# Induced attention and maxout on one core: loads cut into four pieces, two output buffers, a later fetch

## The chip, the cores and the metric

The kernel runs on one core of a Trainium2 chip. The metric is the device time of one execution in microseconds (us), lower is better. TensorE is called PE, ScalarE ACT, VectorE DVE, GpSimd POOL, and SyncE SP, as in the profile. SP issues nearly all transfers (DMAs) of this kernel.

## The reference, cut to what matters

```
B, N, m, C = 4, 12544, 32, 128                      # x: B x N x C, inducing I: m x C
def mab(q, kv):
    s = scale * (q @ kv.transpose(0, 2, 1));  s = s - s.max(-1, keepdims=True)
    a = np.exp(s);  a /= a.sum(-1, keepdims=True) + 1e-09
    return a @ kv
h = mab(I, x)                                       # phase one: 32 rows for each batch
x2 = mab(x, h)                                      # phase two: every token
out = np.maximum(np.maximum(x2 @ w1, x2 @ w2), x2 @ w3) @ w_out    # d_ff = 768
```

All values are float32.

## The kernel before, in words

**Tiles.** Each batch has 98 tiles of 128 tokens, in a short group of 2 tiles and six full groups of 16. The maxout uses `max(w1, w2, w3) = w2 + max(w1 - w2, w3 - w2, 0)` folded with `h`, so that a chunk of up to 512 tokens is worked in six **slots**, one for each block of 128 of the 768 hidden channels. A full group is four chunks, 24 slots, and is called a **window** here; windows are numbered 0 to 23 over the four batches, six a batch, and the short group's chunk stands ahead of each batch's first window.

**A slot.** PE makes two products of the chunk's probabilities `pT` (`pu`, L756; `pv`, L762). ACT turns `pu` into `ru` (a rectifier, L771), DVE takes the maximum with `pv` (`h`, L789), ACT rounds it to a short float (`hi`, L778), and POOL or DVE makes the rest (`lo`, L786, L792). Six slots later PE adds three products into `acc` (L812 to L814, `stage2`; L811 at a chunk's start). After a chunk's last slot, `finish` lets ACT copy `acc` to an output tile `o` (L819), and SP sends `o` to memory (L820, 256 KB).

**What stands beside the slots.** The list `plan` holds for each slot the other steps, put there by `at(slot, step)`. Everything is recorded in this order, and each engine works its own instructions strictly in it. Chunk k's `pT` is written by four DMAs of 64 KB (L741, `probs`) that are recorded in slot 6(k-2)+4; they read `ph` and `pl` of the chunk's group, which ACT (L718) and DVE (L721) write for a whole group at the window's offsets 14 and 15. `ph` and `pl` may be written only when the DMAs that read the tiles before them have landed.

Batches 1 to 3 have their phase one worked during the batch before, a **turn** for each group (windows 0 to 15; 18 turns, two each in windows 0 and 1). With s a turn's first slot, at offset 2 (or 15) of its window: products at s (L363), negated maxima at s+2, `turn_send` at s+4 writes the maxima of 128 rows to memory (`far`, L400, 512 bytes in pieces of 4), `turn_fetch` reads them back so that each row gets four of them (`mm`, L407, 2 KB), and `turn_least`, `turn_weights` and `turn_transpose` follow at s+19 to s+22. `turn_sums` (L446) multiplies the group's tokens in the next window's burst. After a batch's last turn, `turn_totals` and `combine_...` make the next batch's `h`, and `combine_rows` lays its products out by 16 DMAs (`us`, L656, four at each of offsets 18, 20, 22 and 24 of windows 4, 10 and 16).

**Loads.** A group comes twice: with tokens in the partitions (`xg`, L95, 1 MB, `load_tokens`, wanted by `turn_sums`) and with channels there (`xT`, L106, 1 MB, `load_channels`, wanted by the turn's products and later by the scores, L673). For batches 2 and 3 the plan is:

```
at(window(i - 1) + 15, load_channels, n, k)
at(window(i) + 17, load_tokens, n, k)
```

**SP's queue.** The built program gives the DMAs eight semaphores in turn (`DMAHW0` to `DMAHW7`), and a DMA is not issued before the one eight issues earlier has landed. The rows below show it as `[waits DMAHW...]`. SP issues in order, so an issue that waits holds back all behind it.

**The output tile.** `op.tile(..., bufs=3)` asks for three, but the automatic allocation put all 100 at one address: in the built program each copy (L819) waits for the DMA of the chunk just before it.

Of the kernel before, what the change touches and what calls it, by code (L numbers as in the profile page):

```python
# [8 lines left out]
F32 = mybir.dt.float32  # L9
# [16 lines left out]
def kernel(ctx, tc, x, xt, ind_t, w1, w2, w3, w_out, out):  # L26
    nc = tc.nc
    B, N, C = x.shape
    M = ind_t.shape[1]
    DF = w1.shape[1]  # L30
    P = 128
# [3 lines left out]
    GT = 16  # L35
    XB = 5
    XTB = 8
    MANUAL = {mybir.EngineType.PE, mybir.EngineType.Activation, mybir.EngineType.SP, mybir.EngineType.DVE, mybir.EngineType.Pool}

    LOADS = (0, 7, 1, 2, 8, 3, 9, 4, 10, 5)  # L40
# [9 lines left out]
    UW = 2 * DF + C  # L50
# [3 lines left out]
    groups = []  # L54
    t0 = 0
    while t0 < NT:
        nt = NT % GT if t0 == 0 and NT % GT else GT
        assert nt == GT or nt <= NQ
        g = dict(t0=t0, nt=nt, at=t0 * P)
# [8 lines left out]
    const = ctx.enter_context(tc.tile_pool(name="const", bufs=1))  # L68
    xp = ctx.enter_context(tc.tile_pool(name="xp", bufs=2))
    wk = ctx.enter_context(tc.tile_pool(name="wk", bufs=2))  # L70
    bp = ctx.enter_context(tc.tile_pool(name="bp", bufs=2))
    hp = ctx.enter_context(tc.tile_pool(name="hp"))
    op = ctx.enter_context(tc.tile_pool(name="op", bufs=2))
    dp = ctx.enter_context(tc.tile_pool(name="dp", bufs=2, space=bass.MemoryType.DRAM))
    ps = ctx.enter_context(tc.tile_pool(name="ps", bufs=1, space=PSUM))

# [7 lines left out]
    xv = x.rearrange("b (p t) c -> b p t c", t=NT)  # L84


    def load_group(b, gi, pieces=1):
        g = groups[gi]
        if g["nt"] == GT:
            xg = xgs_free.pop(0)  # L90
        else:
            xg = xp.tile([P, g["nt"], C], F32, name="xgs", tag="xgs", bufs=1)
        n = g["nt"] // pieces
        for k in range(0, g["nt"], n):
            nc.sync.dma_start(out=xg[:, k : k + n, :], in_=xv[b, :, g["t0"] + k : g["t0"] + k + n, :])  # L95
        return xg

    def load_group_t(b, gi):
        g = groups[gi]
        n = g["nt"] * P  # L100
        if g["nt"] == GT:
            xT = xts_free.pop(0)
        else:
            xT = short_t[b % 2]
        if b >= B - xt.shape[0]:
            nc.sync.dma_start(out=xT, in_=xt[b - B + xt.shape[0], :, g["at"] : g["at"] + n])  # L106
        return xT

    xg_next = {}
    xts_free = [const.tile([P, GT * P], F32, name=f"xT{i}", tag=f"xT{i}") for i in range(XTB)]  # L110
    xgs_free = [const.tile([P, GT, C], F32, name=f"xg{i}", tag=f"xg{i}") for i in range(XB)]
    w_space = xts_free.pop()
    shelf = const.tile([P, UW + 2 * groups[0]["nt"] * P + 2 * P + 2 * M], F32, name="shelf")
    shelf_at = [0]

    def place(n):
        shelf_at[0] += n
        return shelf[:, shelf_at[0] - n : shelf_at[0]]

    short_t = [place(groups[0]["nt"] * P) for i in range(2)]  # L120
    iT = place(M)

# [8 lines left out]
    def first_loads():  # L131
# [13 lines left out]
        out=sel[:, :M], in_=ident.rearrange("p (q m) -> p m q", m=M), axis=AX.X, op=ALU.add  # L145
    )
    nc.vector.tensor_copy(
        out=sel[:, M:].rearrange("p (q m) -> p q m", m=M),
        in_=sel[:, :M].unsqueeze(1).to_broadcast([P, NQ - 1, M]),
# [88 lines left out]
    state = {}  # L238
# [15 lines left out]
        st["xg"][gi] = xg_next.pop((b, gi))  # L254
        st["xT"][gi] = load_group_t(b, gi)

    def load_tokens(b, k):
        for gi in turns[k]:
            state[b]["xg"][gi] = load_group(b, gi)

    def load_channels(b, k):
        for gi in turns[k]:
            state[b]["xT"][gi] = load_group_t(b, gi)

    def transpose_x(b, gi, k):
        st = state[b]
# [213 lines left out]
    def phase1_first(weights):  # L480

        start_batch(0)
        nc.sync.dma_start(out=iT, in_=ind_t)
        nc.scalar.mul(out=iT, in_=iT, mul=scale)
        first_loads()
        def work(n):
            for _ in range(n):
                next(weights, None)

        def half(gi, k):  # L490
            if gi < NG:
                if k == 0:
                    start_group(0, gi)
                    if gi == NG - 1:
                        start_batch(1)
                        load_channels(1, 0)
                for i in (k, k + 4):
                    transpose_x(0, gi, i)

        start_group(0, 0)  # L500
        transpose_x(0, 0, 0)
        attend_products(0, 0, bank_a[0])
        attend_max(0, 0)
        attend_column(0)
        attend_spread(0, bank_o[0])
        attend_least(0, 0)
        half(1, 0)
        half(1, 8)
        work(4)
        for gi in range(NG - 1):  # L510
            attend_products(0, gi + 1, bank_a[(gi + 1) % 2])
            attend_weights(0, gi)
            half(gi + 2, 0)
            attend_max(0, gi + 1)
            attend_column(0)
            half(gi + 2, 8)
            if gi > 0:
                attend_sums(0, gi - 1, bank_o[1])
                attend_keep(0, gi - 1)
                if xgs_free and (0, NG - 1) not in xg_next and NG - 1 not in state[0]["xg"]:  # L520
                    xg_next[(0, NG - 1)] = load_group(0, NG - 1)
            attend_transpose(0, gi)
            work(WORK[gi][0])
            if gi == NG - 3:
                transpose_w2()
            if gi == NG - 2:
                prep_products()
            attend_spread(0, bank_o[0])
            attend_least(0, gi + 1)
            work(WORK[gi][1])  # L530
        attend_weights(0, NG - 1)
        attend_sums(0, NG - 2, bank_o[1])
        attend_keep(0, NG - 2)
        combine_least(state[0])
        combine_weights(state[0])
        attend_transpose(0, NG - 1)
        combine_mask(state[0])
        sum_groups(state[0])
        attend_sums(0, NG - 1, bank_o[1])
        combine_groups(state[0], range(NG - 1), bank_u[0])  # L540
        total_sums(state[0], bank_o[0])
        attend_keep(0, NG - 1)
        invert_total(state[0])
        combine_groups(state[0], range(NG - 1, NG))
        combine_states(state[0], NQ)
        for _ in weights:
            pass
# [267 lines left out]

    def finish(c):
        at = groups[c.gi]["at"] + (c.q or 0) * c.w
        o = op.tile([P, 512], F32, name="o", tag="o", bufs=3)
        nc.scalar.copy(out=o[:, : c.w], in_=c.acc[:, : c.w])  # L819
        nc.sync.dma_start(out=out[c.b, :, at : at + c.w], in_=o[:, : c.w])  # L820

# [23 lines left out]
    def at(s, f, *args):  # L845
        plan[s].append((f, args))
# [13 lines left out]
    def turn(b, k, s):  # L860

        at(s, turn_products, b, k)
        at(s + 2, turn_max, b, k)
        at(s + 4, turn_send, b, k)
        at(s + 11, turn_fetch, b, k)
        at(s + 19, turn_least, b, k)
        at(s + 20, turn_weights, b, k)
        at(s + 22, turn_transpose, b, k)

    def window(i):  # L870
        return (i // (NG - 1)) * per_batch + short + (i % (NG - 1)) * WIN
# [1 line left out]
    NW = NG - 1  # L873
    FIRST = ((0, 0), (0, 1), (1, 0), (1, 1), (2, 0), (3, 0))
    BURST = (2, 15)
    LOADT = ((0, 0, 0), (0, 0, 1), (0, 5, 2), (0, 15, 3), (1, 16, 4), (2, 15, 5))
    LOADX = ((0, 4, 0), (0, 17, 1), (1, 4, 2), (1, 17, 3), (2, 17, 4), (3, 17, 5))

    for i in range(B * NW):
        b, g = i // NW, i % NW + 1  # L880
# [9 lines left out]
    for n in range(1, B):  # L890
        for k in range(NK):
            if n == 1:
                i, part = FIRST[k]
                then = (i + 1, part)
                if k > 0:
                    at(window(LOADT[k][0]) + LOADT[k][1], load_channels, n, LOADT[k][2])
                at(window(LOADX[k][0]) + LOADX[k][1], load_tokens, n, LOADX[k][2])
            else:
                i, part = NW * (n - 2) + NW - 2 + k, 0
                then = (i + 1, part)  # L900
                if k == 0:
                    at(window(i - 1) + 7, start_batch, n)
                at(window(i - 1) + 15, load_channels, n, k)
                at(window(i) + 17, load_tokens, n, k)
            at(window(then[0]) + BURST[then[1]], turn_sums, n, k)
            at(window(then[0]) + BURST[then[1]] + 1, turn_keep, n, k)
        st = ("state", n)
        s0 = window(NW * n - 2)
        at(s0 + 6, turn_totals, n, bank_a[1])
        at(s0 + 7, invert_total, st)  # L910
        at(s0 + 8, combine_states, st, 1)
        at(s0 + 15, combine_products, n, bank_a[1])
        at(s0 + 15, scores_products, n, 0, bank_a[1][:, UQ : UQ + 2 * M])
        at(s0 + 16, combine_high, st)
        at(s0 + 17, combine_low, st)
        for r in range(NQ):
            at(s0 + 18 + 2 * r, combine_rows, st, r)
        softmax2(n, 0, *(s0 + k for k in (17, 18, 19, 20, 21, 22, 23, 24, 26, 28)))
# [116 lines left out]
```

## Time and profile before

| | |
|---|---|
| time, three runs | 865.87, 865.97, 873.05 us (median 865.97) |
| the profiled execution | 871.83 us, of which the span from the first to the last instruction is 870.0 us |
| granted PE clock over the span | 0.982 |
| PE / ACT / DVE / POOL busy | 94% / 85% / 74% / 73% of the span |
| DMA | 102.54 MB, 118 GB/s on average |

A busy share is an average over the whole span. What a stage is limited by is read from the waits of that stage: which engine stood idle before which instruction, and what ended it. "A <- B" in a row of waits says that A's engine stood idle until B released it.

### The profile page before, as it was taken

The numbers are of one execution on the slowest core, as the hardware profiler recorded it, in microseconds if no ns is written. First come the engines' busy times: TensorE is split into PE (matmuls) and PEld (weight loads), VectorE is DVE, ScalarE is ACT, GpSimd is POOL, SyncE is SP. The second block draws the span as 40 slices with busy tenths as digits, with TensorE's granted clock in tenths as the row PEclk, the third lists the DMA queues.
The fourth block names the chain that finished last, engine by engine and source line by source line (L and its number), as shares of the span: only waits on it lengthen the run. The fifth ranks groups of instructions, "written<-read, shape, count | busy, mean of one in ns | idle before, by whom it ended". The sixth has DMA issues, their size and how long they took to land.

```text
span 870.0 us, 14626 instructions
## 1 busy us (share of the span) xinstructions
PE 819.8 (94%) x4530; PEld 631.8 (73%) x4530; DVE 642.9 (74%) x1112; ACT 741.5 (85%) x1508; POOL 632.3 (73%) x509
## 2 busy tenths in 40 slices
PE   6878999998998998998998999999999999999998
PEld 4645777686776767767766776687777887778786
DVE  6857687686766777867776687687788788778865
ACT  5657798896877889889787897898999999999997
POOL 0037687695776768769677696697788898878887
PEclk9979999999999999999999999999999999999999
DMA  9315552533534245255253433534423222222221
GB/s 347 151 46 185 165 174 74 170 120 101 160 98 146 71 142 166 66 158 157 68 168 95 159 107 106 164 96 130 121 71 103 74 68 67 79 73 73 65 81 49
DMA packets 48813, 102.54 MB, mean 118 GB/s; under 512 B 14304, under 2 KB 18016, under 8 KB 43488
## 3 DMA queue, kind: packets, MB, share of 16 engines
q1 hardware_dynamic: 48736, 101.62, 37.6%
q8 instruction: 36, 0.59, 0.4%
q14 instruction: 41, 0.34, 0.2%
HBM read 48.16 MB, written 25.70 MB: 85 GB/s over the span
## 4 chain that ended last, share of the span: by engine, by line
PE 61%; DMA 20%; ACT 10%; DVE 5%; SPq 2%; issue 2%; POOL 0%; DVEq 0%; ACTq 0%; POOLq 0%
PE pu L756 11%; PE acc L812 11%; PE pv L762 10%; PE acc L813 10%; PE acc L814 10%; DMA pT<-pl 8%; DMA pT<-ph 6%; DMA out_dram<-o 4%; ACT ru L771 4%; ACT hi L778 3%; PE aux L673 3%; DMA xg<-in_x_dram 2%; SPq L741 2%; PE acc L446 2%; PE acc L811 2%; PE aux L363 2%
## 5 line engine op out<-in xcount | busy, mean ns | idle before, releaser
L786 POOL TENSOR_TENSOR lo<-h,hi 128x512 fp32r<-128x512 f32 (+1 forms) x498 | 627.0, 1289 | 180.4 <-ACT hi L778 130.0
L789 DVE TENSOR_TENSOR h<-pv,ru 128x512 f32<-128x512 f32 (+1 forms) x600 | 403.4, 675 | 191.3 <-PE pv L762 107.5
L771 ACT ACTIVATE ru<-pu 128x512 f32<-128x512 f32 (+1 forms) x600 | 369.9, 616 | 63.7 <-PE pu L756 60.1
L778 ACT CAST hi<-h 128x512 fp32r<-128x512 f32 (+1 forms) x600 | 380.6, 634 | 6.9 <-DVE h L789 6.4
L756 PE MATMUL pu<-pT,us 128*128 128x512 f32 (+1 forms) x600 | 236.0, 394 | 32.2 <-DMA pT<-pl 17.5
L812 PE MATMUL acc<-hi,wo_hi 128*128 128x512 f32 (+1 forms) x600 | 236.8, 395 | 0.0
L762 PE MATMUL pv<-pT,us 128*128 128x512 f32 (+1 forms) x600 | 234.8, 391 | 1.9 <-DVE h L789 1.9
L813 PE MATMUL acc<-hi,wo_lo 128*128 128x512 f32 (+1 forms) x600 | 233.1, 389 | 0.0
L814 PE MATMUL acc<-lo,wo_hi 128*128 128x512 f32 (+1 forms) x600 | 232.8, 388 | 0.0
L756 PEld LDWEIGHTS pu<-pT,us 128*128 128x128 f32 x600 | 113.9, 190 | 63.9 <-ACT ru L771 15.2
L812 PEld LDWEIGHTS acc<-hi,wo_hi 128*128 128x128 f32 x600 | 114.0, 190 | 43.4 <-issue 20.9
L762 PEld LDWEIGHTS pv<-pT,us 128*128 128x128 f32 x600 | 114.2, 190 | 27.6 <-DVE h L789 6.2
L814 PEld LDWEIGHTS acc<-lo,wo_hi 128*128 128x128 f32 x600 | 113.8, 190 | 23.5
L813 PEld LDWEIGHTS acc<-hi,wo_lo 128*128 128x128 f32 x600 | 114.0, 190 | 22.3
L819 ACT COPY o<-acc 128x512 f32<-128x512 f32 (+1 forms) x100 | 60.2, 602 | 21.2 <-DMA out_dram<-o 18.1
L792 DVE TENSOR_TENSOR lo<-h,hi 128x512 fp32r<-128x512 f32 x102 | 73.8, 724 | 0.7 <-ACT hi L778 0.7
L811 PE MATMUL acc<-pT,us 128*128 128x512 f32 (+1 forms) x100 | 39.4, 394 | 0.0
L234 POOL TENSOR_TENSOR wo_lo<-xT,wo_hi 128x768 fp32r<-128x768 f32 x1 | 1.8, 1808 | 37.7 <-ACT wo_hi L233 37.7
L673 PE MATMUL aux<-xT,hT 128*32 128x512 f32 x192 | 26.4, 623 | 0.0
L721 DVE TENSOR_TENSOR pl<-aux,ph 128x512 fp32r<-128x512 f32 x24 | 16.5, 688 | 9.9 <-ACT ph L718 9.6
L446 PEld LDWEIGHTS acc<-xg,aT 128*32 128x32 f32 x576 | 16.6, 110 | 8.8 <-issue 4.8
L718 ACT CAST ph<-aux 128x512 fp32r<-128x512 f32 x24 | 14.9, 621 | 9.3 <-DMA pT<-ph 5.0
(132 smaller groups left out, 448.6 us busy)
## 6 DMA issues: line engine op xcount, KB each, us to landing
out_dram<-o SPq DMA_DIRECT2D x96, 256.0 KB
xg<-in_x_dram SPq DMA_DIRECT2D x23, 1024.0 KB
xT<-in_xt_dram SPq DMA_DIRECT2D x18, 1024.0 KB
pT<-ph SPq DMA_DIRECT2D x192, 64.0 KB
pT<-pl SPq DMA_DIRECT2D x192, 64.0 KB
raw<-in_w_dram SPq DMA_DIRECT2D x3, 768.0 KB
us<-uh SPq DMA_DIRECT2D x24, 52.0 KB
us<-ul SPq DMA_DIRECT2D x24, 52.0 KB
```

Of the source, the lines that this page charges most:

```text
L756: nc.tensor.matmul(out=pu[:, :w], lhsT=state[c.b]["us"][:, 2 * j * P : (2 * j + 1) * P], rhs=c.pT[:, :w], start=True, stop=True)
L762: nc.tensor.matmul(out=pv[:, : d.w], lhsT=state[d.b]["us"][:, (2 * j + 1) * P : (2 * j + 2) * P], rhs=d.pT[:, : d.w], start=True, stop=True,)
L771: nc.scalar.activation(out=ru[:, :w], in_=pu[:, :w], func=AF.Relu)
L778: nc.scalar.copy(out=hi[:, : c.w], in_=h[:, : c.w])
L786: nc.gpsimd.tensor_sub(**args)
L789: nc.vector.tensor_max(out=h[:, : d.w], in0=pv[:, : d.w], in1=relus.pop(s)[:, : d.w])
L792: nc.vector.tensor_sub(**low)
L811: nc.tensor.matmul(out=c.acc[:, :w], lhsT=us[:, 2 * DF :], rhs=c.pT[:, :w], start=True, stop=False)
L812: nc.tensor.matmul(out=c.acc[:, :w], lhsT=wo_hi[:, j, :], rhs=c.hh[j][:, :w], start=False, stop=False)
L813: nc.tensor.matmul(out=c.acc[:, :w], lhsT=wo_lo[:, j, :], rhs=c.hh[j][:, :w], start=False, stop=False)
L814: nc.tensor.matmul(out=c.acc[:, :w], lhsT=wo_hi[:, j, :], rhs=c.hl[j][:, :w], start=False, stop=(j == NJ - 1))
L819: nc.scalar.copy(out=o[:, : c.w], in_=c.acc[:, : c.w])
```

## The change: what it does

There are three edits. Every load of tokens or channels of a full group is cut into four DMAs of 256 KB, and the pieces are put at slots of their own (for batches 2 and 3: channels at offsets 5, 8, 11, 14 of the window before the turn's, where one DMA stood at 15; tokens at 7, 12, 17, 22 of the turn's window, where one stood at 17). `o` is no longer a pool's tile: the chunks take two fixed 512-element stretches of the constant tile `shelf` in turn. `turn_fetch` moves from s+11 to s+12. New line numbers: `pT` L763, `xg` L271, `xT` L282, copy L841, output L842, `far` L421, `mm` L428, `us` L678, sums L467.

```diff
-    def load_tokens(b, k):
+    def load_tokens(b, k, piece):
         for gi in turns[k]:
-            state[b]["xg"][gi] = load_group(b, gi)
+            g = groups[gi]
+            if piece == 0:
...
+            n = g["nt"] // PIECES
+            if n or piece == 0:
+                cut = slice(piece * n, (piece + 1) * n) if n else slice(0, g["nt"])
+                nc.sync.dma_start(out=state[b]["xg"][gi][:, cut, :], in_=xv[b, :, g["t0"] :, :][:, cut, :])
...
-        o = op.tile([P, 512], F32, name="o", tag="o", bufs=3)
+        o = outs[c.n % OB]
...
-        at(s + 11, turn_fetch, b, k)
+        at(s + 12, turn_fetch, b, k)
...
-    LOADT = ((0, 0, 0), (0, 0, 1), (0, 5, 2), (0, 15, 3), (1, 16, 4), (2, 15, 5))
-    LOADX = ((0, 4, 0), (0, 17, 1), (1, 4, 2), (1, 17, 3), (2, 17, 4), (3, 17, 5))
+    LOADT = ((0, 0), (0, 1), (0, 13), (0, 17), (1, 17), (2, 5))
+    LOADX = ((0, 5), (0, 17), (1, 5), (1, 17), (2, 9), (3, 7))
...
-                at(window(i - 1) + 15, load_channels, n, k)
-                at(window(i) + 17, load_tokens, n, k)
+                for piece in range(PIECES):
+                    at(window(i - 1) + 5 + 3 * piece, load_channels, n, k, piece)
+                    at(window(i) + 7 + 5 * piece, load_tokens, n, k, piece)
```

`load_channels` is cut in the same way; for batch 1 its pieces stand 2 slots apart and those of the tokens 3 apart, from the offsets in `LOADT` and `LOADX` (window, offset).

**First place: SP's queue in window 13** (a turn of batch 3), from the output of the chunk that ends at offset 6 on. Before:

```order
L820 DMA out_0_dram<-o_6401 128x512 [waits DMAHW4_49,Activation_49]
L400 DMA far_6404<-mq_6371 4x32x1 [waits DMAHW5_49,DVE_49]
L741 DMA pT_6463<-ph_6127 32x512 [waits DMAHW6_49,PE_49]
L741 DMA pT_6463<-pl_6142 32x512 [waits DMAHW7_49]
...
L820 DMA out_0_dram<-o_6497 128x512 [waits DMAHW2_49,Activation_49]
L407 DMA mm_4664<-far_6404 128x1x4 [waits DMAHW5_49,DMAHW3_49]
L106 DMA xT6_92<-in_xt_dram 128x2048 [waits DMAHW4_49]
L741 DMA pT_6559<-ph_6529 32x512 [waits PE_49,Activation_49]
L741 DMA pT_6559<-pl_6544 32x512 [waits DMAHW6_49,DVE_49]
...
L95 DMA xg1_95<-in_x_dram 128x2048 [waits DMAHW1_49]
L820 DMA out_0_dram<-o_6592 128x512 [waits DMAHW2_49,Activation_49]
```

The same place now:

```order
L421 DMA far_6440<-mq_6407 4x32x1 [waits DMAHW3_49,DVE_49]
L271 DMA xg1_92<-in_x_dram 128x512 [waits DMAHW4_49]
L282 DMA xT6_89<-in_xt_dram 128x512 [waits DMAHW5_49,PE_49]
L763 DMA pT_6501<-ph_6163 32x512 [waits DMAHW6_49,PE_49]
...
L282 DMA xT6_89<-in_xt_dram 128x512 [waits DMAHW2_49]
L842 DMA out_0_dram<-shelf_96 128x512 [waits DMAHW3_49,Activation_49]
L271 DMA xg1_92<-in_x_dram 128x512 [waits DMAHW4_49]
L282 DMA xT6_89<-in_xt_dram 128x512 [waits DMAHW5_49]
L428 DMA mm_4642<-far_6440 128x1x4 [waits DMAHW6_49]
L763 DMA pT_6598<-ph_6567 32x512 [waits DMAHW7_49,PE_49,Activation_49]
...
L271 DMA xg1_92<-in_x_dram 128x512 [waits DMAHW3_49]
```

Two pieces now stand between `far` and the four `pT` behind it. The next output is now the eighth issue after `far` and waits for `far`'s semaphore (`DMAHW3` in both rows); before, it was the fifth. Two pieces stand ahead of `mm`, and no 1 MB load stands behind it.

**Second place: SP's queue in window 4**, where `combine_rows` lays out batch 1's products beside the turn of batch 2's first group. Here `xg2` (16 tiles of that group) is loaded, its last piece being this row now:

```order
L842 DMA out_0_dram<-shelf_96 128x512 [waits DMAHW2_49,Activation_49]
L678 DMA us_2734<-uh_2698 32x416 [waits DMAHW3_49,PE_49]
...
L763 DMA pT_2803<-ph_2654 32x512 [waits DMAHW3_49,PE_49]
...
L678 DMA us_2734<-ul_2714 32x416 [waits DMAHW7_49,DVE_49]
...
L271 DMA xg2_93<-in_x_dram 128x512 [waits DMAHW3_49]
L842 DMA out_0_dram<-shelf_96 128x512 [waits DMAHW4_49,Activation_49]
```

Before, the whole load stood ahead of the same output and of all 16 rows of `us`:

```order
L95 DMA xgs_2693<-in_x_dram 128x256 [waits DMAHW4_49]
L95 DMA xg2_96<-in_x_dram 128x2048 [waits DMAHW5_49]
L820 DMA out_0_dram<-o_2709 128x512 [waits DMAHW6_49,Activation_49]
L656 DMA us_2712<-uh_2673 32x416 [waits DMAHW7_49,Pool_49]
L656 DMA us_2712<-uh_2673 32x416 [waits DMAHW0_49]
```

So three of the four pieces have moved ahead, and the last one has moved behind eight `us` rows from `uh`, four `pT`, and four `us` rows from `ul`. Window 10 has the same shape.

More of the change, by code (lines that the diff above doesn't have):

```diff
@@ L37 @@
     XTB = 8
+    OB = 2
+    PIECES = 4
     MANUAL = {mybir.EngineType.PE, mybir.EngineType.Activation, mybir.EngineType.SP, mybir.EngineType.DVE, mybir.EngineType.Pool}
@@ L72 @@
     hp = ctx.enter_context(tc.tile_pool(name="hp"))
-    op = ctx.enter_context(tc.tile_pool(name="op", bufs=2))
     dp = ctx.enter_context(tc.tile_pool(name="dp", bufs=2, space=bass.MemoryType.DRAM))
@@ L112 @@
     w_space = xts_free.pop()
-    shelf = const.tile([P, UW + 2 * groups[0]["nt"] * P + 2 * P + 2 * M], F32, name="shelf")
+    shelf = const.tile([P, UW + 2 * groups[0]["nt"] * P + 2 * P + 2 * M + OB * 512], F32, name="shelf")
     shelf_at = [0]
@@ L118, in place @@
         return shelf[:, shelf_at[0] - n : shelf_at[0]]
+    outs = [place(512) for _ in range(OB)]
     short_t = [place(groups[0]["nt"] * P) for i in range(2)]
@@ L255, in start_group, with load_channels @@
         st["xT"][gi] = load_group_t(b, gi)
-    def load_tokens(b, k):
+    def load_tokens(b, k, piece):
         for gi in turns[k]:
-            state[b]["xg"][gi] = load_group(b, gi)
-    def load_channels(b, k):
-        for gi in turns[k]:
-            state[b]["xT"][gi] = load_group_t(b, gi)
+            g = groups[gi]
+            if piece == 0:
+                if g["nt"] == GT:
+                    state[b]["xg"][gi] = xgs_free.pop(0)
+                else:
+                    state[b]["xg"][gi] = xp.tile([P, g["nt"], C], F32, name="xgs", tag="xgs", bufs=1)
+            n = g["nt"] // PIECES
+            if n or piece == 0:
+                cut = slice(piece * n, (piece + 1) * n) if n else slice(0, g["nt"])
+                nc.sync.dma_start(out=state[b]["xg"][gi][:, cut, :], in_=xv[b, :, g["t0"] :, :][:, cut, :])
+    def load_channels(b, k, piece):
+        for gi in turns[k]:
+            g = groups[gi]
+            if piece == 0:
+                state[b]["xT"][gi] = xts_free.pop(0) if g["nt"] == GT else short_t[b % 2]
+            n = g["nt"] * P // PIECES
+            if g["nt"] == GT or piece == 0:
+                cut = slice(piece * n, (piece + 1) * n) if g["nt"] == GT else slice(0, g["nt"] * P)
+                nc.sync.dma_start(
+                    out=state[b]["xT"][gi][:, cut], in_=xt[b - B + xt.shape[0], :, g["at"] : g["at"] + g["nt"] * P][:, cut]
+                )
     def transpose_x(b, gi, k):
@@ L495, in half @@
                         start_batch(1)
-                        load_channels(1, 0)
+                        for piece in range(PIECES):
+                            load_channels(1, 0, piece)
                 for i in (k, k + 4):
@@ L894 @@
                 then = (i + 1, part)
-                if k > 0:
-                    at(window(LOADT[k][0]) + LOADT[k][1], load_channels, n, LOADT[k][2])
-                at(window(LOADX[k][0]) + LOADX[k][1], load_tokens, n, LOADX[k][2])
+                for piece in range(PIECES):
+                    if k > 0:
+                        at(window(LOADT[k][0]) + LOADT[k][1] + 2 * piece, load_channels, n, k, piece)
+                    at(window(LOADX[k][0]) + LOADX[k][1] + 3 * piece, load_tokens, n, k, piece)
             else:
@@ L901 @@
                 if k == 0:
-                    at(window(i - 1) + 7, start_batch, n)
-                at(window(i - 1) + 15, load_channels, n, k)
-                at(window(i) + 17, load_tokens, n, k)
+                    at(window(i - 1) + 4, start_batch, n)
+                for piece in range(PIECES):
+                    at(window(i - 1) + 5 + 3 * piece, load_channels, n, k, piece)
+                    at(window(i) + 7 + 5 * piece, load_tokens, n, k, piece)
             at(window(then[0]) + BURST[then[1]], turn_sums, n, k)
```

## The prediction

> **What bounds the kernel now.** I read the page's busy shares first, then the two largest rows of what PE waited for from 70 us on (engine, line and releaser, then total us, times, longest).
>
> ```profile
> PE 819.8 (94%) x4530; PEld 631.8 (73%) x4530; DVE 642.9 (74%) x1112; ACT 741.5 (85%) x1508; POOL 632.3 (73%) x509
> ```
>
> ```profile
> PE pu L756 <- DMA pT<-pl: 17.5, 11, 2.4
> PE pu L756 <- ACT ru L771: 11.3, 6, 3.0
> ```
>
> PE is the bound. Of its 870.0 − 819.8 = 50.2 us without work, these rows hold 17.5 + 11.3 = 28.8, and the change, which moves transfers, can bring about that much at best. Next I put two windows side by side (busy us of each engine, the number of instructions in brackets).
>
> ```profile
> core 0: us, PE busy (x) PEld busy (x) DVE busy (x) ACT busy (x) POOL busy (x), PEclk, DMA share, GB/s
> 535.73:569.35 33.62, 31.82 (x174) 24.15 (x172) 24.79 (x43) 29.09 (x59) 25.38 (x21) 1.00 0.43 126
> 600.99:631.65 30.66, 30.66 (x170) 24.56 (x168) 25.37 (x44) 29.06 (x60) 25.69 (x21) 1.00 0.35 103
> ```
>
> The first (window 13) has everything; the second (window 15) has `far`, `mm` and a token load, but no channel load. The first lasts 33.62 us, of which PE worked 31.82, so 1.80 are idle; in the second none are. Where they are lost, the chain of waits says (start, us, what):
>
> ```profile
> 540.05 7.07 DMA pT<-ph
> ...
> 551.09 6.31 DMA pT<-pl
> ...
> 557.49 0.47 PE pu L756
> ```
>
> The chunk's last `pT` DMA took 6.31 us and PE stood 1.80 us for it. SP's timeline of that window (start, us of the issue):
>
> ```profile
> 537.72 0.34 SPq L820 DMA_DIRECT2D out_dram<-o  x1
> 538.15 0.59 SPq L400 DMA_DIRECT2D far<-mq  x1
> ...
> 544.94 0.33 SPq L820 DMA_DIRECT2D out_dram<-o  x1
> 546.65 0.58 SPq L407 DMA_DIRECT2D mm<-far  x1
> 547.28 0.46 SPq L106 DMA_DIRECT2D xT<-in_xt_dram  x1
> ```
>
> `far` was issued at 538.15, and `mm`, which needs it, at 546.65: about 8.5 us for 512 bytes. The third small `pT` behind it, issued at 540.05, landed at 547.12, after `far` too. So what is issued behind `far` completes behind it; three `pT` in the 0.47 us from 546.65 to 547.12 are 0.16 each. The late `pT` of the chain, issued at 551.09, comes behind the 1 MB channel load of 547.28.
>
> **The change part by part.** All sums are against the profiled execution, 871.83 us; it stands 5.86 us above the median of the three runs, 865.97.
>
> *Channel load no longer ahead of the chunk's pT* (17.5 us, 11 stalls). Here is window 15, where that load is absent and PE did not wait:
>
> ```profile
> 602.98 0.34 SPq L820 DMA_DIRECT2D out_dram<-o  x1
> ...
> 615.78 0.59 SPq L741 DMA_DIRECT2D pT<-pl  x1
> ```
>
> Its last `pT` is issued 12.80 us behind the output. In window 13 it was 551.09 − 537.72 = 13.37, and PE wanted it at 557.49 − 1.80 = 555.69, which is 17.97 behind the output. With the change the next output, now eighth behind `far`, waits until `far` has landed, about 8.9 us behind the output; then come the output, two pieces, `mm` and four `pT` at about 0.6 us each: the last `pT` is issued at about 13.3. It has 4.7 us. Bounds: as the 6.31 of the chain, it is 1.6 late and the stalls stay nearly whole; as in window 15, nothing is late. I take window 15, since no 1 MB load is ahead, less a leftover of 0.14 a time for the pieces: −17.5 + 1.5 = **−16.0**.
>
> *Two output buffers.* The chain ahead of a stall at 275.58, then PE's own rows with the idle time in brackets, then ACT's waits:
>
> ```profile
> 265.76 8.87 DMA out_dram<-o
> 274.65 0.58 ACT o L819
> 275.24 0.30 ACT ru L771
> ```
>
> ```profile
> 84.06 0.50 PE L756 MATMUL pu<-pT,us 128*128 128x512 f32 x1 [2.64 <-ACT ru L771]
> 261.78 0.50 PE L756 MATMUL pu<-pT,us 128*128 128x512 f32 x1 [1.66 <-ACT ru L771]
> 275.58 0.39 PE L756 MATMUL pu<-pT,us 128*128 128x256 f32 x1 [2.42 <-ACT ru L771]
> 303.18 0.50 PE L756 MATMUL pu<-pT,us 128*128 128x512 f32 x1 [0.94 <-ACT ru L771]
> 477.14 0.50 PE L756 MATMUL pu<-pT,us 128*128 128x512 f32 x1 [3.04 <-ACT ru L771]
> ```
>
> ```profile
> ACT o L819 <- DMA out_dram<-o: 18.1, 13, 3.3
> ACT ph L718 <- DMA pT<-ph: 5.0, 6, 2.8
> ACT ph L718 <- DMA out_dram<-o: 4.0, 1, 4.0
> ```
>
> The copy at 274.65 stood until the output before it landed at 274.63. The output two chunks back is some 14 us old (two chunks of 7.2 us, by the outputs at 537.72 and 544.94) when its buffer is wanted, more than the 8.87 that one took. So ACT's 18.1 us go; but PE lost only what ACT's slack did not cover, the stalls at 84.06 and 275.58: **−5.1**. Those at 261.78, 303.18 and 477.14, and a small sixth, come from `ph` (the other two rows), which waits for the `pT` behind `far`, and they stay.
>
> *Pieces behind `far`.* Two pieces now stand between `far` and the `pT` that `ph` waits for. ACT reached `ph` this close to its limit:
>
> ```profile
> 302.04 0.59 ACT L718 CAST ph<-aux 128x512 fp32r<-128x512 f32 x1 [1.43 <-DMA pT<-ph]
> 547.19 0.59 ACT L718 CAST ph<-aux 128x512 fp32r<-128x512 f32 x1 [0.27 <-DMA pT<-ph]
> ```
>
> 1.43 us of ACT cost PE 0.94, so some 0.5 is covered; 0.27 cost nothing. A piece behind `far` costs between 0.16 (the `pT` there) and 8.87 (the longest output DMA quoted, of a piece's size, 256 KB); I take 0.3, near the row in the same place. Then `ph` waits 0.27 + 0.6 = 0.87 in an ordinary turn window and PE loses 0.37, and the windows that stall already lose the whole 0.6. Some ten of the one and four of the other: 3.7 + 2.4, less what falls where `ph` has room; **+4** (ends 0, and, at 8.87 a piece, far over a hundred).
>
> *Transitions* (windows 4 and 10). The last piece of the tokens moved behind eight `us`, four `pT` and four `us`. SP's rows in window 4, PE's there, and from the chain the output among the `us` rows:
>
> ```profile
> 229.68 0.62 SPq L820 DMA_DIRECT2D out_dram<-o  x1
> 232.67 6.82 SPq L656 DMA_DIRECT2D us<-uh  x8
> ```
>
> ```profile
> 234.51 0.47 PE L756 MATMUL pu<-pT,us 128*128 128x512 f32 x1 [1.15 <-DMA pT<-pl]
> ...
> 239.67 0.28 PE L446 MATMUL acc<-xgs,aT 128*32 128x128 f32 x2
> ```
>
> ```profile
> 244.66 3.30 DMA out_dram<-o
> ```
>
> `turn_sums` began 9.99 us behind the output, 8.84 without the stall of 1.15; the last quarter of the tokens is wanted some 0.75 later, at 9.6. SP needs 0.62 us for that output and about 0.6 for each of the 16 issues behind it, 10.2 us, before it can issue the piece, which is 0.6 too late without any time to land. With the 3.30 that the output of the same size took there it is 3.9 late; I take 3.0, nearer to that row, which had small DMAs all around it. Two transitions: **+6**. Ends: 0, if PE gets there later than I count, and 2 × 6.9 with a landing like the 6.31 above. What covered this before was the whole load's place ahead of the rows.
>
> *The fetch a slot later.* `mm` goes out with the pieces above and has until the steps at s+19; I cost it at nothing, covered by seven slots. If that cover were gone, DVE's weights, and with them the products of the next burst, would be late by the excess. The added issues (three more for each of some 30 loads, 0.6 us each) are 54 us of SP's time; they fall where SP now stands, as in window 13 from 545.27 to 546.65, when it waited for `far`. Bounds: nothing, and 0.6 for each of the pieces ahead of `mm`, which are in the 13.3 above.
>
> Sum: 871.83 − 16.0 − 5.1 + 4 + 6 = 860.7, a gain of 11.1. From the median this is 865.97 − 11.1 = **854.9 us**. If the 5.86 between the two lies in the stalls themselves, less is to be had, and the range reaches that way.
>
> The pieces are where a rule speaks against the change. The Trainium skill, "DMA: Bandwidth & Descriptors", section "Rules for kernel authors", asks for at least 1 MiB in a DMA for the most bandwidth, and its "Anatomy of one DMA" fits each DMA as 2.0 us and its bytes over 436e3. As an estimate by that page a 256 KB piece takes 2.6 us, and four take 10.4 one after another, where one load takes 4.4. No run here shows 256 KB loads yet; the output of that size above took 3.30 and 8.87, so the page's figure is no worse than the trace. By the rule the third rival below would be the likely one; the 0.16 us of each `pT` behind `far` speaks against it.
>
> **The rivals.** (1) *All that can go goes*: the pieces behind `far` cost nothing and the last token piece lands in time. For it: SP waits where the added issues fall, and window 15 ran with no idle time. Against it: the 10.2 us of issues ahead of the last piece. 871.83 − 17.5 − 5.1 = 849.2, less 5.86: 843.4 us.
>
> (2) *The `pT` wait is renewed*: `far` now holds the next output, so `mm`, the pieces and `pT` leave SP late together, and PE waits for `pT` as before. For it: the last `pT` leaves as late as it did (13.3 against 13.37), and 1.6 of the old 1.80 remain if it takes its 6.31 again. Against it: window 15. Then 871.83 − 17.5 × 0.2 / 1.80 − 5.1 + 4 + 6 = 874.8; with half of the stalls gone, 868.0 (871.83 − 8.75 − 5.1 + 4 + 6). Less 5.86, 862 to 869 us; call it 865. That the change does not do what it says belongs here: were the two stretches of `shelf` guarded as one, the copy would wait for the last output again, which adds 5.1.
>
> (3) *Slower: pieces behind `far` finish one after another.* The place is ACT's `ph` in every turn window. With p us a piece `ph` waits 0.27 + 2p and PE loses 0.5 less, in 14 windows. Without its +4 the sum from the median is 850.9, so it equals the kernel before at 14 × (2p − 0.23) = 15.1, p = 0.65, and is slower by 1% from p = 0.96 on. At p = 1.2, a third of the 3.30 above, it gives 850.9 + 30.4 = 881 us. For it: an output of a piece's size took 3.30 and 8.87. Against it: the `pT` behind `far` needed 0.16 each, since the bytes had moved while `far` was still open.
>
> **How the numbers follow.** The forecast has 0.52 (850 to 860), the first rival 0.15, the second 0.23, the third 0.10. A measurement of this kernel tells about 1% from no change: faster is below 857.3, slower above 874.6. The forecast is below 857.3 seven times in ten, 0.37, the first rival always, 0.15, and the second one time in ten, 0.02: 0.54. Slower holds the third rival nearly whole and the second's far end: 0.11; the rest is 0.35. The range leaves out the lower half of the first rival and most of the third: 843 to 868.
>
> **What would show it.** `pu` <- `pT<-pl` falls from 17.5 to some 1.5; ACT's `o` <- `out_dram<-o` falls from 18.1 to near 0, and the stall of 275.58 is gone; ACT's `ph` waits grow from 9.0 in all to some 17, and PE's waits for `ru` stay at 6 to 10; PE's `acc` (the sums) waits some 3 us for `xg` in windows 4 and 10. The prediction is wrong if `pu` <- `pT` stays above 8, if `ph` waits over 1.3 us on average, or if the sums do not wait at all.

## The result and the profile after

The changed kernel takes 941.61 us (median of four runs, 938.22 to 947.73) where the kernel before took 867.95 beside it: a ratio of 1.085 (95% interval 1.076 to 1.093). The prediction said 854.9, with a range of 843 to 868. Three slow executions are left out of the ratios and intervals in this document: 879.42 and 882.23 us of the kernel before, and 1632.84 us of the changed kernel without `far`. The profiled execution took 944.48 us, with a span of 942.7 us, 72.7 more than before. The page's busy line, and what PE waited for from 70 us on (total us, times, longest):

```profile
PE 848.5 (90%) x4530; PEld 649.7 (69%) x4530; DVE 644.3 (68%) x1112; ACT 744.1 (79%) x1508; POOL 637.4 (68%) x509
```

```profile
PE pu L778 <- ACT ru L793: 46.5, 12, 5.0
PE pv L784 <- DVE h L811: 13.7, 6, 6.2
PE acc L467 <- DMA xg<-in_x_dram: 7.4, 2, 4.2
PE aux L384 <- DMA xT<-in_xt_dram: 5.5, 3, 2.2
PE pu L778 <- DMA pT<-pl: 2.5, 1, 2.5
```

The same 4530 instructions cost PE 28.7 us more of busy time (848.5 against 819.8), and its time without work grew from 50.2 to 94.2, by 44.0; that is the 72.7. PE's waits from 70 us on account for the 44.0 to within 0.5: `ru` +35.2, `h` +11.8, `xg` +7.4, `xT` +5.5, `pT` −15.0 and a row of 0.4 that is gone. The wait for `pT` fell from 17.5 to 2.5, as forecast, but the wait for `ru` quadrupled. Behind it stands ACT, which waited before it could write `ph`:

```profile
ACT ph L740 <- DMA pT<-pl: 34.8, 7, 5.6
ACT ph L740 <- DMA xT<-in_xt_dram: 15.4, 3, 5.4
ACT ph L740 <- DMA pT<-ph: 12.7, 3, 5.3
```

These are 62.9 us in 13 waits, 4.8 each; before they were 9.0 in 7. ACT's wait for its output tile, 18.1 before, has no row any more. Window 13, SP's timeline (the stretch that stood at 537.72 before):

```profile
596.89 0.35 SPq L842 DMA_DIRECT2D out_dram<-shelf  x1
597.33 0.59 SPq L421 DMA_DIRECT2D far<-mq  x1
597.98 0.50 SPq L271 DMA_DIRECT2D xg<-in_x_dram  x1
598.57 0.38 SPq L282 DMA_DIRECT2D xT<-in_xt_dram  x1
599.04 0.53 SPq L763 DMA_DIRECT2D pT<-ph  x1
...
605.62 0.35 SPq L842 DMA_DIRECT2D out_dram<-shelf  x1
608.29 0.33 SPq L271 DMA_DIRECT2D xg<-in_x_dram  x1
609.80 0.52 SPq L282 DMA_DIRECT2D xT<-in_xt_dram  x1
611.03 0.58 SPq L428 DMA_DIRECT2D mm<-far  x1
...
613.96 0.58 SPq L763 DMA_DIRECT2D pT<-pl  x1
```

Each of the four issues from 605.62 to 611.03 waited for the DMA eight issues earlier, so it tells when that one landed: `far` at 605.6, the piece of tokens at 608.3, the piece of channels at 609.8, the first `pT` at 611.0. The third, which `ph` needs, came at 611.37 by the chain, and then:

```profile
611.43 0.58 ACT L740 CAST ph<-aux 128x512 fp32r<-128x512 f32 x1 [5.35 <-DMA pT<-ph]
```

From `far` to that third `pT` it was 0.47 us before and is 5.8 now. The windows view shows the same stretch cut at `far`'s landing, with the part behind it also in two (the last two columns are the busy share of the 16 DMA engines and GB/s):

```profile
core 0: us, PE busy (x) PEld busy (x) DVE busy (x) ACT busy (x) POOL busy (x), PEclk, DMA share, GB/s
599.60:605.60 6.00, 6.00 (x28) 4.95 (x27) 5.21 (x9) 6.00 (x14) 6.00 (x6) 1.00 0.86 34
605.60:611.40 5.80, 1.98 (x9) 1.31 (x7) 0.69 (x1) 0.49 (x1) 2.41 (x2) 0.88 0.72 208
605.60:607.50 1.90, 1.90 (x9) 1.31 (x7) 0.69 (x1) 0.49 (x1) 1.90 (x2) 1.00 0.24 31
607.50:611.40 3.90, 0.08 (x1) 0.00 (x0) 0.00 (x0) 0.00 (x0) 0.51 (x1) 0.81 0.96 294
```

In the 6.0 us before `far` landed, the transfers moved 34 GB/s, some 0.2 of the 0.77 MB that two pieces and four `pT` hold; the view does not say whose bytes these were. The low rate outlasts the landing by 1.9 us (31 GB/s), and then 294 follow. The landings stand in the order of issue: `far`, two pieces, `pT`. So the 512 KB of two pieces land behind 512 bytes, and the `pT` behind them.

The 28.7 us of busy time go with the clock. PE's rows around that stall, and the windows view (PEclk is the third column from the right):

```profile
607.19 0.39 PE L836 MATMUL acc<-lo,wo_hi 128*128 128x512 f32 x1
612.57 0.80 PE L778 MATMUL pu<-pT,us 128*128 128x512 f32 x1 [4.99 <-ACT ru L793]
613.16 0.63 PE L784 MATMUL pv<-pT,us 128*128 128x512 f32 x1
```

```profile
608.00:610.00 2.00, 0.00 (x0) 0.00 (x0) 0.00 (x0) 0.00 (x0) 0.01 (x1) 0.99 1.03 301
610.00:612.00 2.00, 0.00 (x0) 0.00 (x0) 0.00 (x0) 0.57 (x2) 0.00 (x0) 0.50 1.03 364
612.00:614.00 2.00, 1.43 (x3) 1.16 (x4) 1.36 (x3) 2.00 (x6) 0.90 (x1) 0.50 0.39 116
614.00:616.00 2.00, 2.00 (x6) 1.59 (x5) 1.22 (x2) 1.50 (x4) 1.16 (x2) 0.50 0.46 106
616.00:618.00 2.00, 2.00 (x8) 1.58 (x8) 0.81 (x2) 1.55 (x4) 1.05 (x2) 0.80 0.37 116
```

This stall of 4.99 us is paid twice: the clock falls to 0.50 some 2.4 us into it and stays there for over 4 us of work, so a product takes 0.63 us in place of 0.39. Over the span the granted clock fell from 0.982 to 0.950; 870.0 × 0.018 and 942.7 × 0.050 are 15.7 and 47.1 us of full speed, 31 apart; that counts idle time at the low clock too, so it is an upper end for the 28.7.

### The profile page after: what moved, and what is told of

Its sections match the earlier page's. It is cut to its first block, busy times and chain, and to the rows that moved or that the text cites. A ratio compares the mean times of both kernels' runs of the same rounds, so it can differ in the third digit from the quotient of the medians.

```text
span 942.7 us, 14765 instructions
## 1 busy us (share of the span) xinstructions
PE 848.5 (90%) x4530; PEld 649.7 (69%) x4530; DVE 644.3 (68%) x1112; ACT 744.1 (79%) x1508; POOL 637.4 (68%) x509
## 4 chain that ended last, share of the span: by engine, by line
PE 67%; DMA 18%; DVE 5%; ACT 3%; issue 3%; SPq 2%; POOL 1%; DVEq 0%; ACTq 0%; POOLq 0%
PE acc L834 12%; PE pu L778 12%; PE pv L784 12%; PE acc L835 11%; PE acc L836 11%; DMA pT<-pl 6%; DMA xT<-in_xt_dram 4%; DMA pT<-ph 3%; PE aux L695 2%; PE acc L833 2%; DMA xg<-in_x_dram 2%; DMA far<-mq 2%; PE aux L384 2%; SPq L763 2%; PE acc L467 1%
## 5 line engine op out<-in xcount | busy, mean ns | idle before, releaser
L793 ACT ACTIVATE ru<-pu 128x512 f32<-128x512 f32 (+1 forms) x600 | 364.1, 607 | 87.9 <-PE pu L778 83.6
L800 ACT CAST hi<-h 128x512 fp32r<-128x512 f32 (+1 forms) x600 | 375.0, 625 | 8.5 <-DVE h L811 5.8
L778 PE MATMUL pu<-pT,us 128*128 128x512 f32 (+1 forms) x600 | 241.8, 403 | 52.2 <-ACT ru L793 46.5
L784 PE MATMUL pv<-pT,us 128*128 128x512 f32 (+1 forms) x600 | 241.1, 402 | 13.7 <-DVE h L811 13.7
L834 PE MATMUL acc<-hi,wo_hi 128*128 128x512 f32 (+1 forms) x600 | 242.1, 404 | 0.0
L835 PE MATMUL acc<-hi,wo_lo 128*128 128x512 f32 (+1 forms) x600 | 238.1, 397 | 0.0
L836 PE MATMUL acc<-lo,wo_hi 128*128 128x512 f32 (+1 forms) x600 | 237.6, 396 | 0.0
L841 ACT COPY shelf<-acc 128x512 f32<-128x512 f32 (+1 forms) x100 | 59.8, 598 | 3.1 <-PE acc L836 3.1
L384 PE MATMUL aux<-xT,shelf 128*32 128x512 f32 x144 | 25.5, 653 | 5.5 <-DMA xT<-in_xt_dram 5.5
L467 PEld LDWEIGHTS acc<-xg,aT 128*32 128x32 f32 x576 | 16.7, 110 | 16.5 <-DMA xg<-in_x_dram 8.0
```

Of the source, the lines that this page charges most:

```text
L778: nc.tensor.matmul(out=pu[:, :w], lhsT=state[c.b]["us"][:, 2 * j * P : (2 * j + 1) * P], rhs=c.pT[:, :w], start=True, stop=True)
L784: nc.tensor.matmul(out=pv[:, : d.w], lhsT=state[d.b]["us"][:, (2 * j + 1) * P : (2 * j + 2) * P], rhs=d.pT[:, : d.w], start=True, stop=True,)
L793: nc.scalar.activation(out=ru[:, :w], in_=pu[:, :w], func=AF.Relu)
L800: nc.scalar.copy(out=hi[:, : c.w], in_=h[:, : c.w])
L834: nc.tensor.matmul(out=c.acc[:, :w], lhsT=wo_hi[:, j, :], rhs=c.hh[j][:, :w], start=False, stop=False)
L835: nc.tensor.matmul(out=c.acc[:, :w], lhsT=wo_lo[:, j, :], rhs=c.hh[j][:, :w], start=False, stop=False)
```

## The experiments

All ratios are to the kernel before, run on the same chip, with 95% intervals. "Changed" is the kernel with the whole change.

| kernel | ratio | interval |
|---|---|---|
| changed | 1.085 | 1.076 to 1.093 |
| outputs alone | 1.006 | 1.002 to 1.011 |
| outputs, `mq` apart | 0.990 | 0.984 to 0.996 |
| changed, pieces behind the `pT` | 1.030 | 1.022 to 1.037 |
| changed, pieces ahead of `far` | 1.011 | 1.005 to 1.017 |
| changed, one piece left behind `far` | 1.066 | 1.059 to 1.074 |
| changed, `mq` apart | 1.092 | 1.086 to 1.097 |
| changed, `mq` apart, `far` from ACT | 1.069 | 1.063 to 1.075 |
| everything together | 0.986 | 0.980 to 0.993 |
| before, whole loads behind `far` | 1.114 | 1.106 to 1.121 |
| before, outputs, `mq` apart, whole loads early | 0.978 | 0.971 to 0.985 |
| changed, without `far` | 0.967 | 0.960 to 0.974 |
| everything together, without `far` | 0.951 | 0.944 to 0.958 |
| before, outputs, without `far` | 0.957 | 0.952 to 0.963 |

**The place of the pieces.** Three kernels move the pieces that stand between `far` (slot 6 of the window) and the four `pT` recorded at slot 10: all of them behind these, all of them ahead of `far`, and the tokens alone behind these.

```diff
+    def late(o):
+        return o + (11 - o % WIN if 6 < o % WIN < 11 else 0)
+    def early(o):
+        return o - (o % WIN - 5 if 5 < o % WIN < 10 else 0)
-                    at(window(i - 1) + 5 + 3 * piece, load_channels, n, k, piece)
-                    at(window(i) + 7 + 5 * piece, load_tokens, n, k, piece)
+                    at(window(i - 1) + late(5 + 3 * piece), load_channels, n, k, piece)
+                    at(window(i) + late(7 + 5 * piece), load_tokens, n, k, piece)
```

> The changed kernel with every piece that stands between `far` and the four `pT` behind it put behind these (slot 11 of the window). Theory (pieces behind `far` finish one after another, hold the `pT`, so `ph`, so PE): ACT's waits before `ph` fall from 63 us to under 12, the clock stays up, and the time falls from 941 to 855 to 870 us; the transitions keep their 7 us. Rival (256 KB pieces cost the same wherever they stand, by the eight semaphores or by bandwidth): it stays over 920. Second rival (the pieces, now three in a row behind `far` and ahead of `mm`, delay the chunk's `pT` instead): `ph` waits go, but PE's waits for `pT` return at 10 to 30 us, 870 to 890.

> The changed kernel with the pieces between `far` and its `pT` put ahead of `far` (slot 5). Theory: as with the pieces behind the `pT`, `ph` waits under 15 us, 855 to 870 us. If a piece ahead of `far` delays `far` itself as much as one behind it delays `pT`, `ph` waits stay at some 2 to 3 us a window, 890 to 920.

> The changed kernel with the token pieces moved behind the `pT` and the channel pieces left between `far` and `pT`, so that one piece is left there in most turn windows. Theory: the price is per piece; by the landings (2.7 us of the first piece, 1.5 of the second, 1.2 of the first `pT`) `ph` waits some 3 us a window in place of 4.9, and the time lies between, 895 to 925 us. Rival (any piece there gives the whole wait): 935 to 945; rival (only the second counts): under 875.

Measured: 897.76, 881.72 and 930.24 us. ACT's waits in the kernel with the pieces ahead of `far`, and in the one with the channels left behind it:

```profile
ACT ph L740 <- DMA pT<-ph: 10.2, 7, 1.9
ACT ph L740 <- DMA pT<-pl: 7.3, 6, 2.2
```

```profile
ACT ph L740 <- DMA pT<-ph: 33.0, 8, 5.0
ACT ph L740 <- DMA xg<-in_x_dram: 15.2, 4, 4.3
ACT ph L740 <- DMA pT<-pl: 1.0, 1, 1.0
```

So `ph` waits 17.5 us in all with no piece there, 49.2 with one, 62.9 with two: the place is the cause of most of the loss, and the first piece costs more than the second. All three times lie above what was expected of them: 855 to 870 for the first two, and 895 to 925 for the third. What is left with the pieces ahead of `far` has nothing to do with that place: PE still waits 9.6 us for the `xg` of windows 4 and 10, and 16.2 for DVE's `h`, which the next kernels explain. That pieces behind the `pT` do worse (1.030) than ahead of `far` is not the second rival: PE's wait for `pT` is 3.2 there, and it is `xg` (12.2 against 9.6), `xT` (8.7 against 5.1) and `ru` (11.7 against 7.0) that PE waits longer for.

**The outputs.** The kernel before with `o = outs[c.n % OB]` and no output pool, alone, and then with a fixed place for `mq`:

```diff
-        mq = wk.tile([P, 2], F32, name="mq", tag="mq")
+        mq = mqs[0]
+        mqs.append(mqs.pop(0))
```

> The kernel before with two fixed output buffers alone. Our theory: ACT's waits of 18.1 us for its output tile go to near 0, PE loses the two stalls of 2.64 and 2.42 us and no others; 5 us faster than before, up to 8 if the clock no longer drops behind them: 859 to 863 us. Rival (the outputs themselves cause part of the slowdown, by taking semaphores or places of the queue): 870 us or more.

> The kernel before with two fixed output buffers, and the maxima's column `mq` in stretches of its own of the constant tile. Our theory: the output buffers' gain of 5 us was eaten by two waits of 5 to 6 us of DVE's `rs` for `far`, because without the output pool `rs` got the address of `mq`, which `far` reads; with `mq` elsewhere these waits vanish and the kernel is 4 to 10 us faster than the kernel before. Rival (the waits have to do with the outputs' traffic): they stay at some 12 us, and the time stays 3 to 8 us above the kernel before.

Outputs alone: ACT's 18.1 us are gone and PE's wait for `ru` fell from 11.3 to 5.9, and yet the time rose by 0.6%. The waits of PE and of DVE show what took it:

```profile
PE pv L763 <- DVE h L790: 12.1, 4, 5.6
```

```profile
DVE rs L699 <- DMA far<-mq: 12.7, 2, 6.6
```

DVE's `rs`, a column of sums, waited for `far`, with which it has nothing to do. In the built program `rs` waits on the semaphore of `far` at three places, of which those in windows 3 and 7 stall, and nowhere in the kernel before: without the output pool the allocation gave it an address that `far` still reads as `mq`. With `mq` in a stretch of its own the row is gone, and the kernel is 1% faster than before (0.990), the 5 us of the prediction's term and some more. The same edit in the changed kernel:

> The changed kernel with `mq` in stretches of its own, nothing else. Theory: of its excess 13.7 us of PE's waits for DVE's `h` and the slow clock behind them are this address; 14 to 20 us faster than the changed kernel, so some 921 to 930 us. Rival (what waits there is freed only to wait for the pieces behind `far` at the next place): within 5 us of the changed kernel.

It gave nothing (954.34 us, 1.092, where 921 to 930 was expected): PE's wait for `h` fell from 13.7 to 1.9, and that for `ru` rose.

```profile
PE pu L780 <- ACT ru L795: 63.8, 13, 6.2
```

The rival was right: in the changed kernel, where `rs` stalled in windows 3 and 9, the wait for `rs` had stood ahead of the wait for `ph`, and without the first the second is as long.

**Everything together, with `far`.** Pieces ahead of `far`, `mq` apart, a first turn's tokens ahead of the `us` rows, and two channel loads of batch 1 some slots earlier; the line for the third:

```diff
-                    at(window(i) + 7 + 5 * piece, load_tokens, n, k, piece)
+                    at(window(i) + (early(7 + 5 * piece) if k else (5, 11, 12, 14)[piece]), load_tokens, n, k, piece)
```

> Everything together: the changed kernel with the pieces ahead of `far` (slot 5), `mq` apart, the tokens of a batch's first turn at slots 5, 11, 12 and 14, so that all four pieces stand ahead of the `us` rows, and two channel loads of batch 1 some slots earlier. Theory (four causes, each removed): PE's waits for `xg`, `xT`, `h` and `pT` together under 8 us, `ph` still costs about 7; 8 to 18 us faster than the kernel before. Rival (SP or the semaphores are short of room, so one of the waits moves): 0 to 10 us slower than before.

863.05 us, 0.986, within what was expected; PE's waits for `xg` and `xT` are gone. `ph` still waits, and PE waits 19.6 us for `ru` behind it, where some 7 were expected:

```profile
ACT ph L742 <- DMA pT<-ph: 16.9, 7, 6.0
ACT ph L742 <- DMA pT<-pl: 6.1, 4, 2.3
```

**Place or cutting.** The kernel before with its loads whole, once behind `far` and once (the channels) ahead of it:

```diff
-                at(window(i - 1) + 15, load_channels, n, k)
-                at(window(i) + 17, load_tokens, n, k)
+                at(window(i - 1) + 8, load_channels, n, k)
+                at(window(i) + 7, load_tokens, n, k)
```

The second has 5 and 11 in place of 8 and 7, the two edits of outputs and `mq`, and `start_batch` at slot 4 in place of 7.

> The kernel before with its loads whole, one output buffer and all, but for batches 2 and 3 the channels at slot 8 and the tokens at slot 7, between `far` and the four `pT` behind it. It tells the place from the cutting. Theory (place: the bytes behind `far` begin to move only when it has landed, 0.7 MB or 2 MB alike): `ph` waits over 6 us in each of the some 12 windows concerned, 60 to 110 us slower than the kernel before. Rival (the cutting: four small transfers do worse than one large): under 30 us slower.

> The kernel before with two fixed output buffers, `mq` apart, and its loads whole, but for batches 2 and 3 the channels at slot 5, ahead of `far`, and the tokens at slot 11, behind its `pT`. If the cutting brings nothing by itself, this is as fast as the pieces at these places, 8 to 18 us faster than the kernel before; if a whole load ahead of `far` or of the next `pT` delays them by its 5 to 9 us, `ph` or `pT` waits of 2 to 5 us a window make it 10 to 40 us slower.

Behind `far` whole loads lose 11.4%, more than pieces (2 MB stand there, against 512 KB), though the wait shows at `pT` rather than at `ph`, where the expectation had it:

```profile
PE pu L756 <- DMA pT<-pl: 94.5, 12, 10.1
```

The other gains 2.2%, no less than pieces at such places (the intervals of 0.978 and 0.986 overlap). Whole loads lose at the place behind `far` and gain away from it, as pieces do: the place decides, and no harm or help of the cutting itself shows. The slots of the two kernels are not quite the same, so a small effect of the cutting stays open.

**What holds the pieces.** `far` issued by ACT, on a queue of its own (`nc.scalar.dma_start` in place of `nc.sync.dma_start`):

> The changed kernel, pieces where the change put them, with `mq` apart and `far` issued by ACT in place of SP. It tells what holds the pieces. Theory A (the transfers of one queue go in order, and `far` holds those issued behind it by the same engine): the pieces and `pT` land in 2 to 4 us, `ph` waits fall under 10 us, 865 to 885 us. Theory B (the small writes of `far` hold the 16 DMA engines or the memory themselves, whoever issues them): the `ph` waits stay at 50 to 65 us, 920 us or more, plus what ACT loses in waiting for `mq` and in issuing.

The queue table shows it on a queue of its own, and the windows view of window 13 shows the same picture as above:

```profile
q10 hardware_dynamic: 2376, 0.01, 0.2%
```

```profile
593.60:599.60 6.00, 6.00 (x28) 4.95 (x28) 5.14 (x9) 6.00 (x14) 6.00 (x6) 1.00 1.00 36
599.60:604.90 5.30, 2.83 (x13) 2.01 (x11) 1.48 (x3) 1.37 (x4) 3.25 (x3) 1.00 0.74 205
```

Theory B held so far as it says that the issuing engine does not matter: until `far` landed, by SP's next issue at 599.7, the transfers moved 36 GB/s, and 205 behind it; ACT waits 58.5 us for `ph`; the time is 935.18 us. Another queue is no way around it (from 1.092 to 1.069). Whether it is the DMA engines or the memory that `far` holds was not settled. Last, `far` and `mm` taken away, with the maxima spread over the rows by a small product, as `attend_spread` does it for the first batch:

```diff
-        nc.sync.dma_start(out=far[0].rearrange("(m q) -> q m", q=NQ), in_=far[1])
+        nc.vector.tensor_scalar(out=md, in0=quad, scalar1=st.pop(("mq", k)), scalar2=None, op0=ALU.mult)
...
-        nc.sync.dma_start(out=st["mm"][:, k, :NQ], in_=every)
+        nc.tensor.matmul(out=mp, lhsT=sel, rhs=md, start=True, stop=True)
+        nc.vector.tensor_copy(out=st["mm"][:, k, :NQ], in_=mp)
```

> The changed kernel, every piece where the change put it, but without `far` and `mm` transfers: the maxima are spread over the rows by a product on PE (128 x 4, at s+7), as the first batch does it. Theory (`far` is what holds all transfers behind it, pieces and `pT` alike): ACT's waits for `ph` fall from 63 us to under 5, and only the waits for `xg` and `xT` (13 us) and some 5 us of the new products remain, 5 to 15 us faster than the kernel before. Rival (the pieces are slow because of the eight semaphores or their number, and `far` only stands ahead of them): `ph` waits stay over 30 us and the time over 905.

> The same without `far`, and with the pieces moved as in the kernel that has everything together (ahead of slot 6, a first turn's tokens ahead of the `us` rows, two loads of batch 1 earlier). Theory: PE waits for under 5 us in all behind 70 us; it had 31.6 in the kernel before, and the products cost some 5: 20 to 30 us faster than the kernel before. Rival (PE has no room for 18 more products and DVE's two operations each): no faster than the kernel with everything together, 8 to 12 us faster than before.

> The kernel before with two output buffers and its loads whole at their old places, with the maxima spread by the product on PE in place of `far` and `mq`'s fetch. It tells what the pieces bring once `far` is gone, beside the kernel with pieces and the product (0.967 of the kernel before). If the pieces bring what the prediction gave them (the end of the `pT` waits behind a channel load of 1 MB, 16 us), this one keeps some 10 to 17 us of `pT` waits and stands at 0.98 to 0.99; if those waits too were `far`'s work, since `mm` and `pT` left late behind it, they go here as well, and it stands at 0.95 to 0.97.

With the pieces exactly where the change put them the time is 848.96 us (0.967), 26 us faster than before where 5 to 15 were expected, and no row of ACT for `ph` is left. (`mm`, issued at 611.03 in window 13 above, left too late to have held these `pT`, so it is `far` that did.) PE's busy line and its longest wait:

```profile
PE 814.6 (96%) x4566; PEld 629.9 (75%) x4566; DVE 656.4 (78%) x1148; ACT 740.2 (88%) x1508; POOL 634.3 (75%) x509
```

```profile
PE acc L469 <- DMA xg<-in_x_dram: 8.1, 2, 4.2
```

With the pieces moved as well it is 835.11 us (0.951), 40 us faster where 20 to 30 were expected. The kernel before with its loads whole at their old places and without `far` takes 837.19 (0.957; the two intervals overlap), and this is all that PE waits for there from 70 us on:

```profile
PE pv L765 <- DVE h L792: 1.9, 3, 0.7
PE aux L409 <- DVE hT L601: 1.7, 2, 0.9
PE aux L480 <- DVE a L382: 0.5, 2, 0.3
```

The 17.5 us for `pT` are gone, though the channel load of 1 MB stands ahead of them as before. They too were `far`'s work. Part of it is that `mm`, the load and `pT` left late behind it: in two windows with a channel load the last `pT` is now issued 12.1 and 12.0 us behind the output (516.92 − 504.84, 548.58 − 536.57), in place of 13.37.

## Why the prediction was wrong, point by point

- **The failed step is the price of a piece behind `far`**, put at 0.3 us "near the row in the same place". It was (5.8 − 0.47) / 2, some 2.7 us. The row near it was a `pT` of 64 KB, and its 0.16 us was read as the price of a place in the queue; the prediction wrote that the bytes had moved while `far` was still open. For the `pT` of before that was so, as these rows of its window 13 show, where `far` is open to the end. The first is 0.27 MB, about what the four `pT` hold, and the second next to nothing:

```profile
540.00:542.50 2.50, 2.50 (x13) 2.07 (x12) 2.12 (x4) 2.50 (x7) 2.50 (x3) 1.00 0.50 108
542.50:545.00 2.50, 2.50 (x12) 2.07 (x12) 2.14 (x5) 2.50 (x6) 2.50 (x3) 1.00 0.02 3
```

  With the pieces there, some 0.2 of 0.77 MB moved in the 6.0 us before `far` landed, and most came behind it. The other end of the bound, the 8.87 us of an output of the same size, was the better guide. The term was +4; PE's wait for `ru` alone rose by 46.5 − 11.3 = 35.2, though the two output stalls in it had gone.
- **The third rival** had the right mechanism, place and sign, with a chance of 0.10. Its own formula with 2.7 a piece gives 850.9 + 14 × (5.4 − 0.23) = 923 us; it was priced at 1.2. Its 0.65, from which it decides, was passed four times over. The prediction's own estimate of 2.6 us a piece comes near the 2.7 by luck: it leaves `far` out, and without `far`, with the same pieces at the same places, `ph` does not wait at all.
- **The clock was left out of the sum.** A stall was counted at its length, though before the change, too, a stall over 2.3 us had been followed by half the clock. The first two rows are around the stall of 2.35 us that ended at 413.04 in the profile of before, and the third follows the 2.64 that ended at 84.06, where the fall came only behind the stall:

```profile
411.00:413.00 2.00, 0.00 (x0) 0.00 (x0) 0.00 (x0) 1.10 (x4) 2.00 (x2) 0.99 0.93 293
413.00:415.00 2.00, 1.96 (x5) 1.60 (x6) 0.66 (x1) 1.10 (x2) 0.02 (x1) 0.50 0.59 188
84.00:86.00 2.00, 1.94 (x10) 0.46 (x10) 1.38 (x2) 2.00 (x6) 1.41 (x2) 0.82 0.58 160
```

  In window 13 of before, 1.80 us had left it at 1.00. The Trainium skill, "TensorE: Matmul & The Clock Gate", section "HAM oscillation — how this bites in real kernels", gives as the rule that gaps stay below some 3.4 us. Here a gap of 2.35 us was enough.
- **The output buffers**, −5.1, were right in themselves (PE's wait for `ru` fell by 5.4 with them alone), and were eaten by an address that nothing in the diff shows.
- **The `pT` term**, −16.0, came out at −15.0, for a reason that is only half the one given: `far` kept it late, and the size of the load behind `far` only added to it. The way there was not the forecast's either: the last `pT` is issued 613.96 − 596.89 = 17.07 us behind the output, not 13.3, because the issues before it waited for landings and the first `pT` for `ph`; that is later even than the second rival had it. PE had just stood 4.99 us at `ru`, so that a late `pT` cost it little, and that part is luck; with the pieces ahead of `far`, where PE waits only 7.0 for `ru`, the `pT` wait is 2.1, so the term itself holds.
- **The transitions**, +6, came out at +7.4, 3.2 and 4.2 us for the `xg` of windows 4 and 10. The 5.5 us for `xT` in batch 1's turns had no term.
- **The later fetch**, at nothing, was not tried by itself.

## What to carry to other kernels

Look for the transfer that lands late for its size before moving any other: here 512 bytes took 8 us, everything issued behind them waited, and the stalls showed under other names (`pT`, `ph`, an output tile). When it can't be seen what a new neighbour costs behind such a transfer, the bound belongs to a neighbour of the same bytes, not to the nearest small one. And a tile pool that is taken away moves addresses: the waits of the built program, set beside those of before, show a new dependency where the diff has none.

## What the runs showed of the hardware

- `far`, 512 bytes written to memory in pieces of 4, took 8.3 us in window 13 of the changed kernel (605.62 − 597.33). What SP issued behind it landed behind it. In the last 6.0 us that it was open the transfers moved 34 GB/s (36 in the kernel where ACT issued it), with 0.77 MB and more behind it. In window 13 of before, with 0.26 MB behind it, 0.27 MB moved in 2.5 us (108 GB/s) and next to nothing in the next 2.5, and the third `pT` still landed only behind it. Why it takes that long was not settled: no run wrote the same bytes in larger pieces.
- PE's granted clock fell to 0.50 some 2.4 us into a stall of 4.99 us, and products of 0.39 us then took 0.63 for over 4 us of work. After a stall of 2.64 us it fell about 1.2 us behind the stall's end (0.82 over 84 to 86), and after one of 1.80 us it stayed at 1.00.
